# Reading K and V of two batches with the keys in another order: a source with 8 outer rows in place of 128

## The chip, the cores and the metric

The kernel runs on one core of a Trainium2 chip. The metric is the device time of one execution in microseconds; three runs of the kernel before have a median of 851.9 us. Lower is better. Times inside an execution are counted from the start of the profiled span.

## What is computed

Two attention blocks stand side by side, and their outputs are joined in the last dimension. Both have 16 batches of 32 query tokens, a model width of 1024, 32 query heads of width 128 and a cache of 1024 keys. Block A has 4 key/value heads, each shared by 8 query heads; block B has a key/value head for every query head. All inputs are bf16.

```python
q = (x @ wq).reshape(B, Sq, H, Dh).transpose(0, 2, 1, 3)
k, v = repeat(k_cache, rep, axis=1), repeat(v_cache, rep, axis=1)   # rep 8 in A, 1 in B
p = softmax(einsum("bhqd,bhkd->bhqk", q, k) * Dh ** -0.5)
o = einsum("bhqk,bhkd->bhqd", p, v)
out = o.transpose(0, 2, 1, 3).reshape(B, Sq, H * Dh) @ wo           # A and B, then concatenate
```

Softmax and the sum over keys don't depend on the order of the keys, as long as K and V have the same one.

## The kernel before

The program is written as a list of operations (matrix groups on TensorE, evictions from PSUM on VectorE or ScalarE, transfers issued by SyncE), each with the buffers that it reads and writes. A planner, `list_schedule`, gives every engine a fixed order, from a duration for each operation; a transfer's duration comes from its size (`dur`, in bytes) and its packets' length. Semaphores are put where an operation depends on one of another engine. SP carries all loads in one order, and waits before a load until the buffer that it overwrites is free.

The work of A runs in four blocks of heads, and in each block over the 16 batches in order: a batch brings one K tile and one V tile of A (1024 keys by 128, 256 KB), and its two halves (`q.half`) use them for 4 query heads each. So there are 64 K tiles and 64 V tiles of A in the run. Two buffers each hold them, by `q.b % 2` (`KA_sb`, `VA_sb`). Each is `[128 partitions, 8 chunks, 128]`, and partition p holds the keys 8p to 8p+7, 2 KB that lie together in DRAM:

- `st_dmaKA` (L885) and `st_dmaVA` (L892) issue the loads on SP.
- `st_ktrA` transposes the 8 chunks of K on TensorE (L963); the result is evicted to `KTA_sb`.
- `st_scoresA` multiplies by the queries (L989), `st_max` (L1029, VectorE) and `st_exp` (L1042, ScalarE) do the softmax's parts, `st_ptr` (L1054) transposes the probabilities, and `st_pvA` (L1074) multiplies them by V, chunk by chunk.

Chunk c of the transposed K therefore holds key 8p + c in column p, and chunk c of V has the same key on partition p.

Block B streams larger tiles: 512 KB for two heads, loaded at L904 (K) and L949 (V), in 4 KB rows. K of B is transposed on VectorE in place (L970), its scores are L1018 and its product with V is L1108. The weights of the queries (`wq`, L708) and of the outputs (`wo`, L789 and L799) are loaded between them. In the last steps some tiles of B are put into the buffers of `wq`, `xT` and `QT`, which are free by then.

Of the kernel before, what the change touches and what calls it, by code (L numbers as in the profile page):

```python
# [16 lines left out]
NVB_SLOTS = 6  # L17
XT_FREE = 54
LATE = 51
NQT = 5  # L20
NKB_SLOTS = 8
LAZY_PER_STEP = 100
# [524 lines left out]
def build(nc, pa, pb, out):  # L547
# [9 lines left out]
    NCH = Sk // P  # L557
# [22 lines left out]
    pr = Prog()  # L580
    stack = contextlib.ExitStack()
    with stack:
        def sb(name, shape, dt):
            return stack.enter_context(nc.sbuf_tensor(name, shape, dt))
# [9 lines left out]
        QT_sb = sb("QT_sb", [P, 2, Bn, HS, Sq], BF)  # L594
        Qtok = sb("Qtok", [P, NQT, CW], BF)
        QBt = sb("QBt", [P, CW], BF)
# [8 lines left out]
        KA_sb = sb("KA_sb", [P, 2, NCH, Dh], BF)  # L605
        VA_sb = sb("VA_sb", [P, 2, NCH, Dh], BF)
# [11 lines left out]
        def bank(v):  # L618
            return psum[:, v.idx, :]
# [17 lines left out]
        def evac(dst_ap, src_ap, reads, writes, name, eng=None, wtag=None, rtag=None, mul=None):  # L637
            def emit(e):
                dst = dst_ap() if callable(dst_ap) else dst_ap
                src = src_ap() if callable(src_ap) else src_ap  # L640
                if mul is not None:
                    if hasattr(e, "activation"):
                        return e.activation(dst, src, ACTF.Copy, scale=mul)
                    return e.tensor_scalar(dst, src, mul, None, ALU.mult)
                return e.copy(dst, src) if hasattr(e, "activation") else e.tensor_copy(dst, src)  # L645
            eng = eng or "any"
            pr.add(eng, emit, reads=reads, writes=writes, name=name if eng == "any" else name + "@" + eng, wtag=wtag, rtag=rtag)
# [66 lines left out]
        def wq_reads(pi, c, j0, j1):  # L714
            return [r_ for k_ in sorted(set(j * WQP // DJ for j in range(j0, j1))) for r_ in wq_res(pi, c, k_)]
# [22 lines left out]
        def qprojB(m_, G):  # L738
# [5 lines left out]
            for j0 in range(0, DJ, JS):  # L744
                def e_qp(e, j0=j0):
                    last = None
                    for j in range(j0, j0 + JS):
                        last = e.matmul(bank(v)[:, 0:CW], xT_sb[:, 1, j, G * P:(G + 1) * P], wq_sb[:, j, mh * CW:(mh + 1) * CW], start=(j == 0), stop=(j == DJ - 1))  # L748
                    return last
                ws = wq_reads(1, c2, j0, j0 + JS)  # L750
                pr.add("pe", e_qp, reads=ws + [("xT", 1, G)] + ([("xV", 0), ("xV", 1)] if m_ == NMSB - 1 else []), writes=[v], claims=[("Qtok", (m_ * NG + G) % NQT)], name="qprojB", dur=0.225 * JS,
                       rtag=dict((r_, ("wq", 1, c2)) for r_ in ws))
            qs = (m_ * NG + G) % NQT
            evac(Qtok[:, qs, :], lambda: bank(v)[:, 0:CW], reads=[], writes=[v, ("Qtok", qs)], name="qB_ev",
                 wtag={("Qtok", qs): (m_, G)}, mul=scale)

        def qprepB_tr(m_, G):
            qs = (m_ * NG + G) % NQT
            pr.add("dve", lambda e: e.transpose(QBt[:, :].bitcast(F32), Qtok[:, qs, :].bitcast(F32)),
                   reads=[("Qtok", qs)], writes=["QBt"], name="QBt_tr", rtag={("Qtok", qs): (m_, G)}, wtag={"QBt": (m_, G)})  # L760
# [103 lines left out]
        def mk_quadB(t):  # L864
# [13 lines left out]
            q.kid = ("B", t)  # L878
            return q

        def st_dmaKA(q):
            if not q.kv_new:
                return
            sl = q.kvslot
            pr.add("sp", lambda e: e.dma_start(KA_sb[:, sl, :, :], pa["k"][q.b, q.s].rearrange("(p c) d -> p c d", c=NCH)),  # L885
                   writes=[("KA", sl)], dma_key=f"ka{sl}", name="ka_dma", dur=Sk * Dh * 2, wtag={("KA", sl): q.kid})

        def st_dmaVA(q):
            if not q.kv_new:
                return  # L890
            sl = q.kvslot
            pr.add("sp", lambda e: e.dma_start(VA_sb[:, sl, :, :], pa["v"][q.b, q.s].rearrange("(p c) d -> p c d", c=NCH)),  # L892
                   writes=[("VA", sl)], dma_key=f"va{sl}", name="va_dma", dur=Sk * Dh * 2, wtag={("VA", sl): q.kid})

        def tile_src(key, x):
# [4 lines left out]
        def st_dmaKB(x):  # L900
            if x < 2 * NIT:
                kind, sl = home_k(x)
                pr.step, was = 2 * ((x - NKB) // 4) if x >= NKB else pr.step, pr.step
                pr.add("sp", lambda e: e.dma_start(tile_k(x), tile_src("k", x)), writes=[(kind, sl)], dma_key=f"{kind.lower()}{sl}", name="kb_dma",  # L904
                       dur=2 * Sk * Dh * 2, wtag={(kind, sl): x})
                pr.step = was

        V_LAST = 2 * NIT - 4

        XK = 4 * LATE + 4 + NKB  # L910
        XV = 4 * LATE + 4 + 2

# [33 lines left out]
        def st_dmaVB(x):  # L946
            kind, sl = home_v(x)
            pr.step, was = 2 * ((x - NVB) // 4) if x >= NVB else pr.step, pr.step
            pr.add("sp", lambda e: e.dma_start(tile_v(x), tile_src("v", x)), writes=[(kind, sl)],  # L949
                   dma_key=f"{kind.lower()}{sl}", name="vb_dma", dur=2 * Sk * Dh * 2, wtag={(kind, sl): ("V", x)})  # L950
            pr.step = was
# [48 lines left out]
        def st_scoresB(qs):  # L1000
            n = qs[0].pn
            vP, vPT = (("xT", 0, 0), ("xT", 0, 1)) if n >= XT_FREE and n % 2 else (Virt("P2"), Virt("PT2"))
            for q in qs:
                score_buf(q)
                q.vP, q.vPT, q.vO = vP, vPT, Virt("O2")
            q0 = qs[0]
            gp = (q0.m * NG + q0.G) % 2

            def e_s(e, fp):
                last = None  # L1010
                o0 = (fp // 2) * 64 + fp % 2
                for x in range(4):
                    for q in qs:
                        for g2 in range(2):
                            r0 = 32 * (2 * q.e + g2)
                            lhsT = QR[r0:r0 + 32, gp, 2 * q.bp + x // 2, x % 2, o0:o0 + 63:2]
                            rhs = tile_k(4 * q.pn + x)[r0:r0 + 32, :].rearrange("p (s x) -> p s x", s=16)[:, :, o0:o0 + 63:2]
                            last = e.matmul(bank(q.vS[g2])[32 * x:32 * x + 32, :].rearrange("p (s j) -> p s j", s=16), lhsT, rhs,  # L1018
                                            start=(fp == 0), stop=(fp == 3), tile_position=(r0, 32 * x))
                return last  # L1020
            qr = [("QR", gp, 2 * q0.bp + t_) for t_ in range(2)]
            kt = [(home_k(4 * q0.pn + x), ("T", 4 * q0.pn + x)) for x in range(4)]
            for fp_ in range(4):
                pr.add("pe", lambda e, fp_=fp_: e_s(e, fp_), reads=qr + [r_ for r_, _ in kt], writes=[r_ for q in qs for r_ in q.vS],
                       name="scoresB", tag="B%d" % q0.t, rtag=dict([(r_, (q0.m, q0.G)) for r_ in qr] + kt))
# [67 lines left out]
        def st_pvB(qs):  # L1093
            q0 = qs[0]
            vPT = q0.vPT
            gp = (q0.m * NG + q0.G) % 2
            vt = [home_v(4 * q0.pn + x) for x in range(4)]

            def e_pv(e, c0):
                last = None  # L1100
                pt = pt2_of(vPT).rearrange("p (m r two) -> p m r two", m=8, two=2)
                for c in range(c0, c0 + 4):
                    for t_ in range(2):
                        assert vt[2 * t_ + 1] == (vt[2 * t_][0], vt[2 * t_][1] + 1)
                        v2 = tiles_v(4 * q0.pn + 2 * t_, 2).rearrange("p i (s d) -> p i s d", s=16)
                        for q in qs:
                            e0, n0 = 64 * q.e, 64 * t_
                            last = e.matmul(bank(q.vbo)[n0:n0 + 64, 0:2 * Dh].rearrange("p (i d) -> p i d", i=2), pt[e0:e0 + 64, c // 2, n0:n0 + 64, c % 2],  # L1108
                                            v2[e0:e0 + 64, :, c, :], start=(c == 0), stop=(c == 15), tile_position=(e0, n0))
                return last  # L1110
            for c0 in range(0, 16, 4):
                pr.add("pe", lambda e, c0=c0: e_pv(e, c0), reads=[vPT] + vt, writes=[q.vbo for q in qs], claims=[("OT", 1, gp, h_) for h_ in range(MS)],
                       name="PVB", tag="B%d" % q0.t, rtag=dict((r_, ("V", 4 * q0.pn + x)) for x, r_ in enumerate(vt)))
# [88 lines left out]
        def pairB(n):  # L1202
# [6 lines left out]
            st_scoresB(qs)  # L1209
            while k_next[0] < min(2 * NIT, 4 * n + 4 + NKB + (4 if n >= LATE else 0)):  # L1210
                st_dmaKB(k_next[0])
# [11 lines left out]
            st_pvB(qs)  # L1223
            while v_next[0] < min(V_LAST, 4 * n + 4 + NVB + (4 if n >= LATE else 0)):
                st_dmaVB(v_next[0])
# [35 lines left out]
        for x in range(4):  # L1261
            st_dmaKB(x)
        st_dmaKA(quadsA[newA[0]])
        st_dmaVA(quadsA[newA[0]])
        for x in range(4):
            st_dmaVB(x)
# [86 lines left out]
        if SCHED:  # L1353
            pr = pr.list_schedule()
# [41 lines left out]
```

## Time and profile before

| | |
|---|---|
| three runs | 851.47, 851.9, 852.7 us |
| the profiled execution | 851.77 us |
| its span, first to last instruction | 850.0 us |
| granted TensorE clock in it | 0.998 |
| read from HBM | 337.6 MB |
| DMA packets | 112,208; 341.68 MB |
| loads of K and V of A | 64 and 64, 256 KB each, 8.4 and 8.7 us from issue to landing |
| loads of K and V of B | 256 and 256, 512 KB each |

The profile's page gives busy times of the engines, the span in 40 slices, the DMA queues, and the chain of work that ended last, followed back from the last instruction. In its groups a line reads: line, engine, operation, output <- inputs, count. Waits are given as who waited <- for whom: us in total, how often, the longest. The queue q1 carries the loads and stores that SP issues, q8 and q14 the instructions of the engines themselves, in blocks, and q0 the stores issued by GpSimd. The trace also holds every DMA packet with its start, length, size and queue, but not the number of its DMA engine, and the time of each semaphore increment: a transfer makes sixteen, and has landed with the last.

### The profile page before, as it was taken

Reading aid. Unit: us, or ns where it says so; the run is one execution under the profiler, and the core shown is the slowest. Engines: PE = TensorE matmul, PEld = TensorE weight load, DVE = VectorE, ACT = ScalarE, POOL = GpSimd, SP = SyncE. Lnnn points to the kernel's source line nnn. Section 1 sums busy time; section 2 is a strip of 40 time slices with the busy share of each in tenths; the row PEclk is TensorE's granted clock in tenths of the full one; section 3 lists DMA queues with packets and bytes.
Section 4 is the critical chain, followed back from the end, with each engine's and each line's share of the span. In section 5 each row is a group of like instructions: output and inputs, shape, how many; then the busy total and the mean of one; then the engine's idle time right before and its main releaser. Section 6 shows DMA issues by size and latency. Waiting matters only on the chain.

```text
span 850.0 us, 29762 instructions
## 1 busy us (share of the span) xinstructions
PE 781.1 (92%) x13056; PEld 519.9 (61%) x13056; DVE 734.1 (86%) x1025; ACT 622.9 (73%) x1356; POOL 6.1 (1%) x20
## 2 busy tenths in 40 slices
PE   6988989999899999999998998999999998989886
PEld 3456666666666566676565665566656666666654
DVE  1499898897898899998999789998899889998995
ACT  3378887876778767877777777686777758787864
POOL 1000000000000000000000000000000000000000
PEclk9999999999999999999999999999999999999999
DMA  9999999999999999999999999999999999999994
GB/s 331 415 404 411 412 411 416 415 400 354 409 414 411 415 412 411 415 397 413 408 416 414 413 406 403 415 403 414 413 404 411 410 411 407 416 415 414 416 417 187
DMA packets 112208, 341.68 MB, mean 402 GB/s; under 512 B 12048, under 2 KB 12304, under 8 KB 112080
## 3 DMA queue, kind: packets, MB, share of 16 engines
q1 hardware_dynamic: 111520, 337.95, 99.8%
q8 instruction: 103, 1.69, 0.7%
q0 software_dynamic: 560, 1.84, 0.5%
q14 instruction: 25, 0.20, 0.1%
HBM read 337.64 MB, written 2.10 MB: 400 GB/s over the span
## 4 chain that ended last, share of the span: by engine, by line
PE 53%; DVE 17%; DMA 15%; ACT 12%; issue 2%; SPq 1%; DVEq 0%; ACTq 0%
PE psum L1108 10%; PE psum L817 9%; DVE stat L1029 8%; ACT P_sb L1042 7%; DVE KB_sb L970 6%; DMA KB_sb<-in_B_k_cache_dram 6%; DMA VB_sb<-in_B_v_cache_dram 5%; PE psum L1018 5%; PE psum L1054 5%; PE psum L748 4%; PE psum L1088 4%; PE psum L989 4%; PE psum L729 4%; PE psum L1074 3%; PE psum L963 2%; DMA wq_sb<-in_B_k_cache_dram 2%
## 5 line engine op out<-in xcount | busy, mean ns | idle before, releaser
L1029 DVE TENSOR_REDUCE stat<-psum 128x1 f32<-128x1024 f32 x256 | 302.9, 1209 | 42.2 <-PE psum L989 25.3
L1042 ACT ACTIVATE P_sb<-psum,stat 128x1024 bf16<-128x1024 f32 x246 | 275.2, 1119 | 70.7 <-DVE stat L1029 67.8
L970 DVE STREAM_TRANSPOSE KB_sb<-KB_sb 128x1024 f32<-128x1024 f32 x240 | 289.7, 1226 | 17.3 <-DMA KB_sb<-in_B_k_cache_dram 16.8
L645 ACT COPY PT_sb<-psum 128x512 f32<-128x512 f32 x223 | 129.5, 598 | 39.7 <-PE psum L1088 22.2
L1108 PE MATMUL psum<-VB_sb,PT_sb 64*64 64x256 bf16 x3584 | 116.9, 271 | 11.9 <-ACT P_sb L1042 6.9
L1108 PEld LDWEIGHTS psum<-VB_sb,PT_sb 64*64 64x64 bf16 x3584 | 96.6, 107 | 33.0 <-issue 29.5
L1167 ACT ACTIVATE O_sb<-psum,stat 128x128 bf16<-128x128 f32 (+1 forms) x203 | 80.8, 418 | 35.4 <-PE psum L1074 16.1
L1054 PE MATMUL psum<-id,P_sb 128*128 128x128 f32 x512 | 88.5, 296 | 4.3 <-ACT P_sb L1042 3.0
L989 PE MATMUL psum<-KTA_sb,QT_sb 128*128 128x512 bf16 x256 | 82.0, 383 | 5.8 <-ACT P_sb L1042 2.6
L1054 PEld LDWEIGHTS psum<-id,P_sb 128*128 128x128 f32 x512 | 73.7, 208 | 19.5 <-ACT P_sb L1042 7.9
L1074 PE MATMUL psum<-VA_sb,PT_sb 128*128 128x128 bf16 x1024 | 77.8, 219 | 4.6 <-ACT P_sb L1042 1.9
L1088 PE MATMUL psum<-id,P_sb 128*128 128x128 f32 x472 | 78.1, 288 | 4.1 <-ACT P_sb L1042 1.1
L1074 PEld LDWEIGHTS psum<-VA_sb,PT_sb 128*128 128x128 bf16 x1024 | 62.5, 98 | 28.3 <-issue 12.3
L1018 PE MATMUL psum<-KB_sb,QR 32*32 32x512 bf16 x3840 | 72.7, 395 | 6.2 <-ACT P_sb L1042 5.4
L1088 PEld LDWEIGHTS psum<-id,P_sb 128*128 128x128 f32 x472 | 64.8, 193 | 20.1 <-ACT PT_sb L645 4.5
L748 PE MATMUL psum<-wq_sb,xT_sb 128*128 128x512 bf16 x256 | 73.0, 392 | 3.3 <-DMA wq_sb<-in_B_wq_dram 2.8
L817 PE MATMUL psum<-woB_sb,OTB_sb 128*128 128x512 bf16 x256 | 66.3, 380 | 3.6 <-ACT P_sb L1042 1.6
L817 PE MATMUL psum<-woA_sb,OTA_sb 128*128 128x512 bf16 x256 | 62.8, 380 | 2.2 <-ACT P_sb L1042 1.9
L1018 PEld LDWEIGHTS psum<-KB_sb,QR 32*32 32x32 bf16 x3840 | 43.6, 89 | 32.5 <-ACT P_sb L1042 9.8
L729 PE MATMUL psum<-xT_sb,wq_sb 128*128 128x512 bf16 x192 | 53.3, 379 | 0.5 <-ACT P_sb L1042 0.3
L1042 ACT ACTIVATION_READ_ACCUMULATOR P_sb<-psum,stat 128x1 f32 x246 | 49.6, 202 | 0.0
L829 DVE TENSOR_TENSOR acc<-acc,psum 128x512 f32<-128x512 f32 x64 | 41.2, 674 | 4.2 <-PE psum L817 4.2
(74 smaller groups left out, 718.3 us busy)
## 6 DMA issues: line engine op xcount, KB each, us to landing
KB_sb<-in_B_k_cache_dram SPq DMA_DIRECT2D x240, 512.0 KB, 9.6
VB_sb<-in_B_v_cache_dram SPq DMA_DIRECT2D x234, 512.0 KB, 9.2
KA_sb<-in_A_k_cache_dram SPq DMA_DIRECT2D x64, 256.0 KB, 8.4
VA_sb<-in_A_v_cache_dram SPq DMA_DIRECT2D x64, 256.0 KB, 8.7
wq_sb<-in_B_wq_dram SPq DMA_DIRECT2D x16, 512.0 KB, 8.1
woB_sb<-in_B_wo_dram SPq DMA_DIRECT2D x32, 256.0 KB, 9.8
woA_sb<-in_A_wo_dram SPq DMA_DIRECT2D x32, 256.0 KB, 10.0
wq_sb<-in_B_k_cache_dram SPq DMA_DIRECT2D x16, 512.0 KB, 11.4
```

The lines of the kernel that those rows point to most:

```text
L645: return e.copy(dst, src) if hasattr(e, "activation") else e.tensor_copy(dst, src)
L748: last = e.matmul(bank(v)[:, 0:CW], xT_sb[:, 1, j, G * P:(G + 1) * P], wq_sb[:, j, mh * CW:(mh + 1) * CW], start=(j == 0), stop=(j == DJ - 1))
L817: last = e.matmul(bank(v)[:, 0:OUTW], OT[:, gp, hh, :], wo_[:, hh, oh * OUTW:(oh + 1) * OUTW], start=(hh == 0), stop=(hh == nh - 1))
L970: pr.add("dve", lambda e: e.transpose(tile_k(x).bitcast(F32), tile_k(x).bitcast(F32)), writes=[home_k(x)], name="KBt_tr", rtag={home_k(x): ...
L989: pr.add("pe", lambda e, u=u: e.matmul(bank(vS[u]), qt[:, q.b, q.hh0:q.hh0 + 4, :].rearrange("p a q -> p (a q)"), KTA_sb[:, sl, u * 512:(u ...
L1018: last = e.matmul(bank(q.vS[g2])[32 * x:32 * x + 32, :].rearrange("p (s j) -> p s j", s=16), lhsT, rhs, start=(fp == 0), stop=(fp == 3), t ...
L1029: pr.add("dve", lambda e: e.tensor_reduce(stat[:, vst.idx, 0:1], both(vS), AXIS.XY, ALU.max, negate=True), writes=vS + [vst], name="max")
L1042: return e.activation(dst, src, ACTF.Exp, bias=stat[:, vst.idx, 0:1], scale=1.0, accum_out=stat[:, vst.idx, 1:2])
L1054: last = e.transpose(bank(vb)[:, m * P:(m + 1) * P], p32[:, m:Sk // 2:NPK], id32[:])
L1074: last = e.matmul(bank(vb)[:, 0:Dh], ptc_of(vPT, c, 0, P), VA_sb[:, kvs, c, :], start=(c == 0), stop=(c == NCH - 1))
L1088: last = e.transpose(bank(vb)[:, m * P:(m + 1) * P], p32[:, 4 * h + m:Sk:8], id32[:])
L1108: last = e.matmul(bank(q.vbo)[n0:n0 + 64, 0:2 * Dh].rearrange("p (i d) -> p i d", i=2), pt[e0:e0 + 64, c // 2, n0:n0 + 64, c % 2], v2[e0:e ...
```

## The change

For the batches b with b % 8 == 3 (3 and 11), the K and V tiles of A are read with the keys in another order. With x from 0 to 7 and v from 0 to 15, partition 16x + v gets the keys 64v + 8x to 64v + 8x + 7. The source is then an array with 8 outer rows (a step of 2 KB), 16 inner ones (a step of 16 KB) and 2 KB that lie together. K and V have the same order, so the result stays. The destination is written as 128 partitions of 1024 numbers for all batches. Nothing else is changed; sizes, buffers, waits and names are as before.

```diff
+EIGHT = (3,)
...
+        def a_src(key, q):
+            src = pa[key][q.b, q.s]
+            if q.b % 8 in EIGHT:
+                return src.rearrange("(v x c) d -> x v (c d)", x=8, c=NCH)
+            return src.rearrange("(p c) d -> p (c d)", c=NCH)
+
         def st_dmaKA(q):
...
-            pr.add("sp", lambda e: e.dma_start(KA_sb[:, sl, :, :], pa["k"][q.b, q.s].rearrange("(p c) d -> p c d", c=NCH)),
+            pr.add("sp", lambda e: e.dma_start(KA_sb[:, sl, :, :].rearrange("p c d -> p (c d)"), a_src("k", q)),
                    writes=[("KA", sl)], dma_key=f"ka{sl}", name="ka_dma", dur=Sk * Dh * 2, wtag={("KA", sl): q.kid})
 
         def st_dmaVA(q):
...
-            pr.add("sp", lambda e: e.dma_start(VA_sb[:, sl, :, :], pa["v"][q.b, q.s].rearrange("(p c) d -> p c d", c=NCH)),
+            pr.add("sp", lambda e: e.dma_start(VA_sb[:, sl, :, :].rearrange("p c d -> p (c d)"), a_src("v", q)),
                    writes=[("VA", sl)], dma_key=f"va{sl}", name="va_dma", dur=Sk * Dh * 2, wtag={("VA", sl): q.kid})
```

## The prediction

> **What bounds the kernel now.** I read the page first: engines, DMA rows, chain.
>
> ```profile
> PE 781.1 (92%) x13056; PEld 519.9 (61%) x13056; DVE 734.1 (86%) x1025; ACT 622.9 (73%) x1356; POOL 6.1 (1%) x20
> DMA  9999999999999999999999999999999999999994
> q1 hardware_dynamic: 111520, 337.95, 99.8%
> q8 instruction: 103, 1.69, 0.7%
> PE 53%; DVE 17%; DMA 15%; ACT 12%; issue 2%; SPq 1%; DVEq 0%; ACTq 0%
> KA_sb<-in_A_k_cache_dram SPq DMA_DIRECT2D x64, 256.0 KB, 8.4
> VA_sb<-in_A_v_cache_dram SPq DMA_DIRECT2D x64, 256.0 KB, 8.7
> ```
>
> TensorE is 92% busy and the DMA engines are busy from end to end: two limits of nearly one height. The waits and the chain say which of them counts where. Waits for a landing, from 60 to 570 us and then from 570 us to the end (us in total, times, longest):
>
> ```profile
> DVE KB_sb L970 <- DMA KB_sb<-in_B_k_cache_dram: 11.8, 16, 2.0
> PE psum L1108 <- DMA VB_sb<-in_B_v_cache_dram: 2.6, 5, 0.7
> PE psum L817 <- DMA woB_sb<-in_B_wo_dram: 0.4, 1, 0.4
> ```
>
> So 14.8 us of waiting, in pieces of about 0.7 us, and almost all before 570 us. The chain (start, us, what) still passes through a transfer every 16 to 140 us, and the last one is what the end hangs on:
>
> ```profile
> 102.47 7.99 DMA VB_sb<-in_B_v_cache_dram
> 140.08 9.15 DMA VB_sb<-in_B_v_cache_dram
> 167.01 12.71 DMA KB_sb<-in_B_k_cache_dram
> ...
> 553.90 6.19 DMA KB_sb<-in_B_k_cache_dram
> 686.25 9.94 DMA woB_sb<-in_B_wo_dram
> 812.16 14.65 DMA wq_sb<-in_B_k_cache_dram
> 826.84 1.25 DVE wq_sb L970
> ```
>
> The last K tile lands at 826.81 us, DVE takes it at once, and 23 us of work follow to 850.0.
>
> **What a landing waits for.** A transfer has landed when its sixteen semaphore increments are in. For that last K tile they come at 821.89 us plus 0, 0.02, 0.15, 0.51, 0.78, 0.96, 1.02, 1.20, and then 2.92, 2.93, 3.42, 3.57, 3.74, 3.92, 4.27, 4.92 us: eight DMA engines are through early, eight run behind, and the last sets the landing. The median spread over all transfers is 3.3 us. The packet records say why. Packets of one engine follow each other at a fixed pitch (2 KB every 80 ns, 4 KB every 155 ns), so each can be tied to the one that starts where it ended. Besides the data there are the 103 instruction blocks of 16 KB (q8 above, 0.935 us each); their lengths repeat with a period of eight, so they go round eight engines, and the two that I could measure alone threw their engine back by 1.41 and 1.40 us. Over the run that is 103 / 8 x 1.41 = 18.1 us on each of eight engines and none on the other eight.
>
> **The change, part by part.** Dependences, sizes and the planner's durations (`dur=Sk*Dh*2`) stay, so all five instruction orders stay. No instruction is added on PE, DVE or ACT: the keys' order inside a tile differs, but K and V share it.
>
> *The transfers.* Batches 3 and 11 are read once in each of four blocks: 8 K and 8 V transfers, 16 in all. Every transfer of before uses 16 engines (11,936 closing packets for 746 transfers), 8 packets of 2 KB each here, 0.646 us. One with an outermost 8 is not in the trace. Two ends: it is dealt over 16 as before and nothing changes, or its eight groups go to eight engines, 16 packets each. I take eight, since the dealing goes by rows now and there are eight outer ones. An engine then needs 1.29 us: the row for it is the weight load of wq, 16 packets of 2 KB per engine, which land 1.29 us apart, and which also step through DRAM with gaps (2 KB of every 8 KB), as the new source does (2 KB of every 16 KB). So each transfer puts 0.646 us more on eight engines and takes 0.646 us from the others: 16 x 0.646 = 10.3 us each way.
>
> [...]
>
> *Which eight.* In the first transfer eight increments come within 0.08 us, the other eight 0.47 to 0.66 us later: engines are served in two halves. Three of the later half then idle for 2 us and stay 1.7 us behind the rest; the first instruction block (23.4 us) falls on one of these three. The second and third fall on engines that a stall at 54 us puts into the same later half: there eight engines stop after 4 or 5 of a transfer's 8 packets, the other eight after 3 or not at all. So the blocks ride on the half that is served second. A transfer that needs only eight is nearest to the row in which the first half is served first; I take that half, the free one.
>
> *The sum.* Loaded engines: 18.1 - 10.3 = 7.8 us behind an ideal one; free engines: 0 + 10.3. The larger falls from 18.1 to 10.3: 7.8 us less, the most that can come of it. The least is nothing: where queues run dry (185 to 210 us, and about 54, 370, 550, 625 and 700 us) compute sets the pace and the lag is reset. For what counts I take the stretches separately. After the dry point at 700 us the chain's end is a landing: one K and one V transfer of batch 11 (issued at 730 and 755 us) lie in it, 2 x 0.646 = 1.3 us off the last engine, whole on the path. Before that, 6.5 us of relief remain, and 14.8 us of waits in short pieces, about eleven of them on the chain (11 x 0.67 = 7.4 us); behind each of them PE's own order is late next. I take 0.3 of the 6.5, 2.0 us, because PE is 92% busy. Together 3.3 us: the profiled execution took 851.77 us (span 850.0), 0.1 below the median of 851.9, so 848.6.
>
> *Costed at nothing.* The changed transfers themselves land up to 0.65 us later on the free engines. Between landing and first use (L963 for K, L1074 for V) the 64 K tiles have a median of 15 us and the 64 V tiles 9.3; of the sixteen the tightest is a V at 477.8 us, used 1.35 us later. If the slack were gone it would cost 0.65 us each. SP's issues (0.33 to 0.45 us) may grow for a three-level source; SP spends some 430 us waiting for PE to free buffers, so 16 x 0.2 us hide there, and what queues behind is the next load with 8 to 10 us to its landing.
>
> **Rivals.**
>
> *The eight are the loaded ones (slower).* Then 18.1 + 10.3 = 28.4 us on the worst half. For it: no view names an engine, and my tying rests on three blocks. Against: three out of three. It decides from the first pair on (40 us), since that half is already the last. At the same share of what reaches the path (3.3 of 7.8) 10.3 us give 4.4: 856.2. Chance 0.15.
>
> *The eight get in others' way (slower).* Each of eight engines writes a run of 16 partitions, where now each writes eight. If packets slow as far as the slowest in the trace, the instruction blocks (16 KB in 0.935 us against 0.62 for four of 4 KB, a factor 1.5), a transfer takes 1.93 us: the free half gets 16 x 1.29 = 20.6 us, over the 18.1 of now, and the others' gain goes in the collisions. It decides from a factor of 1.38 (16 x 0.646 x (2 x 1.38 - 1) = 18.1). 2.5 us, in jumps of 2.6 us per pair, which I count in full: 854.3. Against: strided 2 KB packets in wq keep 80 ns. Chance 0.14.
>
> [...]
>
> *Hidden anyway (no change).* Compute sets the time everywhere but in the tail, and there the V tiles, landing at 839.87 us and used at 840.49, keep the end. 851.5. For: no wait of note after 570 us. Against: the chain's last link but DVE's is a landing. Chance 0.10.
>
> *It doesn't do what it says.* All 16 engines are used still: 851.9. Chance 0.02.
>
> **Numbers.** The forecast has 0.59. A measurement of this kernel tells about 0.2%, 1.7 us, from no change. Faster by more: 0.59; within: 0.10 + 0.02 = 0.12; slower: 0.15 + 0.14 = 0.29. The likeliest case's own range is 844.1 (all 7.8 us) to 850.6 (the tail alone). The range cuts little off below, 845.0, and reaches the loaded-half case, 856.2, above.
>
> **What would show it.** Right: the packet count stays 112,208 but the sixteen transfers' engines close with 16 data packets; the two groups of eight increments close up, with a spread at the last K landing under 3.5 us instead of 4.9; that landing comes before 825.5 us; the waits of L970 for KB fall under 9 us. Wrong in its half: the spread grows to 6 us or more. Wrong in its pace: increments of KA and VA of these batches, or those behind them, more than 1.4 us apart from their neighbours on one engine. Wrong in the share: the landings move forward, but PE's waits take the time back.

## The result: 29 us slower

The changed kernel takes 880.81 us (four runs, 879.68 to 882.32), the one before 851.69 in the same set of runs. The ratio is 1.0341, 95% interval 1.0321 to 1.036: slower by 3.4%. The profiled execution took 880.12 us, 878.3 of it in the span. Here and below a difference in microseconds is the ratio less one, times the median of before in the same set; here 0.0341 x 851.69 = 29.0.

Engines, DMA rows and chain of the profile after:

```profile
PE 787.8 (90%) x13056; PEld 523.1 (60%) x13056; DVE 736.8 (84%) x1025; ACT 623.1 (71%) x1356; POOL 6.1 (1%) x20
DMA  9999999999999999999999999999999999999994
DMA packets 112080, 341.68 MB, mean 389 GB/s; under 512 B 11920, under 2 KB 12176, under 8 KB 111952
q1 hardware_dynamic: 111392, 337.95, 99.5%
q8 instruction: 103, 1.69, 0.7%
PE 46%; DMA 25%; DVE 14%; ACT 10%; SPq 2%; issue 2%; DVEq 0%; ACTq 0%
KA_sb<-in_A_k_cache_dram SPq DMA_DIRECT2D x64, 256.0 KB, 9.2
VA_sb<-in_A_v_cache_dram SPq DMA_DIRECT2D x64, 256.0 KB, 9.4
```

The packets before:

```profile
DMA packets 112208, 341.68 MB, mean 402 GB/s; under 512 B 12048, under 2 KB 12304, under 8 KB 112080
```

Same bytes, and the DMA engines as busy as before, for 28 us longer: they move less in their busy time (389 GB/s, 402 before). 128 packets are missing, 16 x 8: each changed transfer closes on eight engines in place of sixteen. Nearly every kind of load takes longer to land (the 240 K tiles of B 10.4 us, 9.6 before), and the chain passes through transfers for 25% of the span, before 15%.

The longest waits for a landing from 60 to 570 us (us in total, times, longest; the lines of the loads and behind them have moved by 7, L817 by 1), and below from 570 us to the end:

```profile
DVE KB_sb L977 <- DMA KB_sb<-in_B_k_cache_dram: 27.1, 27, 3.0
PE psum L1115 <- DMA VB_sb<-in_B_v_cache_dram: 4.3, 3, 2.8
PE psum L818 <- DMA woB_sb<-in_B_wo_dram: 2.9, 2, 2.2
```

```profile
DVE KB_sb L977 <- DMA KB_sb<-in_B_k_cache_dram: 7.0, 12, 1.2
PE psum L1115 <- DMA VB_sb<-in_B_v_cache_dram: 3.2, 2, 2.8
```

34.3 us in the first stretch where 14.4 had been, and 10.2 in the second, which had 0.4. Transfers of B, which the change doesn't touch, are nearly all of the late ones: for tiles of A, TensorE waits 1.7 us in both stretches together, before not at all. From the chain (start, us, what):

```profile
427.23 10.27 DMA VB_sb<-in_B_v_cache_dram
458.29 9.28 DMA KB_sb<-in_B_k_cache_dram
482.86 13.58 DMA VA_sb<-in_A_v_cache_dram
...
820.42 14.74 DMA KB_sb<-in_B_k_cache_dram
835.18 1.25 DVE KB_sb L977
```

The link at 482.86 us is a changed transfer, the one at 458.29 was issued 0.7 us behind a changed one (K, 457.61 us). That one by stretches (stretch, its length, busy us of each engine, granted clock, DMA share, GB/s):

```profile
455.00:460.00 5.00, 4.76 (x113) 3.54 (x111) 5.00 (x8) 4.73 (x11) 0.00 (x0) 1.00 1.01 413
460.00:463.00 3.00, 2.12 (x28) 1.48 (x31) 3.00 (x4) 2.81 (x7) 0.00 (x0) 1.00 0.98 298
463.00:464.00 1.00, 1.00 (x44) 1.00 (x42) 1.00 (x3) 1.00 (x3) 0.00 (x0) 1.00 1.01 401
464.00:466.00 2.00, 2.00 (x40) 1.39 (x29) 1.51 (x5) 2.00 (x6) 0.00 (x0) 1.00 1.08 336
466.00:471.00 5.00, 3.25 (x26) 1.90 (x24) 3.54 (x6) 2.21 (x5) 0.00 (x0) 1.00 1.02 407
```

Twice the rate falls, to 298 and to 336 GB/s, with the DMA engines busy all the time. The trace's semaphore increments tell why twice. The transfer ahead, the changed one and the one behind (us):

```
ahead    459.98 460.04 460.10 460.19 460.30 460.32 460.36 460.42 460.55 460.72 461.46 461.61 462.30 462.41 464.01 464.69
changed  462.14 462.27 462.42 462.44 462.62 462.77                                                         465.84 466.61
behind   462.99 463.04 463.09 463.17 463.44 463.48 463.51 463.67 463.68 463.69 463.70 463.72 463.94 464.03 466.99 467.57
```

Six of the eight engines do their part between 460 and 462.8 us; the other two are the two that were last already, and do it from 464 us on. And in both stretches the 4 KB packets are long, also those of engines that have no part in the changed transfer: their median is 159 ns from 456 to 460 us, 211 in the microsecond from 461, 159 again at 462 and 463, 213 and 208 from 464 and 465, and 159 from 466 on; a few last over 1 us. All 67 that start from 464.75 to 465.75 us last 194 ns or more. So there are two things to explain: packets that lengthen on every engine, and the last engine's double work. Summed over all engines from 20 us on, what data packets last beyond 159 ns (4 KB) and 84 ns (2 KB) is 176 engine-us in the profile before and 582 after. The rise is bunched at the sixteen changed transfers: 342 of the 582 lie in the 110 us in which these are carried out (each from 2.4 us before its first engine's increment to 0.2 us behind the last), and the other 750 us have 240. Divided by sixteen engines the rise is 406 / 16 = 25.4 us. Below this rise, so divided, is called the lengthening of a run.

TensorE's granted clock fell too: 0.986 to 0.990 in the four runs, 0.998 in the profile before. In the profile after it stands at a half four times, for 17.0 us in all (from 76.2, 287.8, 472.1 and 694.0 us), and in the four microseconds ahead of each TensorE had been idle for 2.0 to 2.8 us; before, it stands at a half once within the work, for 3.4 us. TensorE's busy time grew by 6.7 us (781.1 to 787.8), half of the 13.6 us more. Ahead of 472.1 us the chain leads from the late K tile above (landed at 467.57 us) over DVE and ACT to TensorE, idle from 469.2 to 471.2 us. So up to some 6.7 of the 29 us may be a slower TensorE behind longer waits; no run here tells this part from the rest.

### The profile page after: what moved, and what is told of

Same layout as the page of the kernel before. It is cut to its first block, busy times and chain, and to the rows that moved or that the text cites. A ratio compares the mean times of both kernels' runs of the same rounds, so it can differ in the third digit from the quotient of the medians.

```text
span 878.3 us, 29762 instructions
## 1 busy us (share of the span) xinstructions
PE 787.8 (90%) x13056; PEld 523.1 (60%) x13056; DVE 736.8 (84%) x1025; ACT 623.1 (71%) x1356; POOL 6.1 (1%) x20
## 4 chain that ended last, share of the span: by engine, by line
PE 46%; DMA 25%; DVE 14%; ACT 10%; SPq 2%; issue 2%; DVEq 0%; ACTq 0%
DMA KB_sb<-in_B_k_cache_dram 16%; PE psum L818 8%; PE psum L1115 8%; ACT P_sb L1049 6%; DVE stat L1036 6%; DVE KB_sb L977 5%; DMA VB_sb<-in_B_v_cache_dram 5%; PE psum L1025 5%; PE psum L1061 4%; PE psum L730 4%; PE psum L1095 4%; PE psum L749 3%; PE psum L996 3%; PE psum L1081 3%; PE psum L970 2%
## 5 line engine op out<-in xcount | busy, mean ns | idle before, releaser
L977 DVE STREAM_TRANSPOSE KB_sb<-KB_sb 128x1024 f32<-128x1024 f32 x240 | 291.3, 1230 | 38.8 <-DMA KB_sb<-in_B_k_cache_dram 38.3
L1115 PE MATMUL psum<-VB_sb,PT_sb 64*64 64x256 bf16 x3584 | 120.1, 276 | 18.5 <-ACT P_sb L1049 7.5
L1115 PEld LDWEIGHTS psum<-VB_sb,PT_sb 64*64 64x64 bf16 x3584 | 99.2, 109 | 39.8 <-issue 36.3
## 6 DMA issues: line engine op xcount, KB each, us to landing
KB_sb<-in_B_k_cache_dram SPq DMA_DIRECT2D x240, 512.0 KB, 10.4
```

The costliest lines, as they stand in the source:

```text
L977: pr.add("dve", lambda e: e.transpose(tile_k(x).bitcast(F32), tile_k(x).bitcast(F32)), writes=[home_k(x)], name="KBt_tr", rtag={home_k(x): ...
```

## Experiments

Three theories of the lengthening and the lateness: *writes* (a source with few outer rows gives each engine a run of neighbouring partitions, which takes it to where other engines write), *reads* (2 KB of every 16 KB, read side by side), *load* (eight engines simply have double work). In all runs the orders of PE, DVE, ACT and POOL are those of before.

**Other reading, same outer 8.**

```diff
-                return src.rearrange("(v x c) d -> x v (c d)", x=8, c=NCH)
+                rows = pa[key].rearrange("b s (g c) d -> (b s g) (c d)", c=NCH)[128 * (4 * q.b + q.s):]
+                return rows[:136].rearrange("(x v) e -> x v e", x=8)[:, :16]
```

> The sixteen transfers keep an outermost source dimension of 8, but each engine now reads sixteen adjacent 2 KB pieces, and the next engine starts 34 KB further on (17 pieces, so that the two source dimensions can't be merged; up to 7 of the 128 pieces of these two batches come from the tile behind, and the keys of these batches are other ones). Writes theory (what slows all engines is that each of eight writes a run of 16 partitions, out of its usual place): unchanged, 881. Reads theory (it is the reading of 2 KB every 16 KB by engines that walk side by side): the lengthened packets go, and the time is between my forecast and before, 848.6 to 852. Load theory (eight engines simply have double the work, and they are the wrong eight): 881 as well, with the spread of the increments as in the changed kernel.

880.03 us, ratio 1.0335 (1.0311 to 1.0358); lengthening 23.8 us. Each engine reads 32 KB that lie together, and nothing is gained. The reads theory falls; the other two had both forecast this.

**Strided reading, outer 128.**

```diff
-                return src.rearrange("(v x c) d -> x v (c d)", x=8, c=NCH)
+                n = 4 * q.b + q.s
+                return pa[key].rearrange("b s (g c) d -> (b s g) (c d)", c=NCH).rearrange("(r p j) e -> r j p e", p=128, j=8)[n // 8, n % 8]
```

> The sixteen transfers keep an outermost dimension of 128 and so sixteen engines in their usual dealing; only the source steps by 16 KB per partition (one piece of 2 KB out of each 16 KB, over eight tiles; the keys of these two batches are other ones). Reads theory: as slow as the changed kernel or slower, 875 to 885, since all sixteen engines read with the step. Writes theory and load theory: 852, as before.

851.68 us, ratio 1.0015 (0.9998 to 1.0033); lengthening 0.1 us. The step of 16 KB costs nothing that shows.

**The old order in two halves.**

```diff
+            return [e.dma_start(dst[h:h + 64], src[h:h + 64]) for h in (0, 64)] if cut else e.dma_start(dst, src)
```

> The sixteen transfers in their old key order, each as two transfers of 64 partitions (0 to 63, then 64 to 127) on one semaphore: sixteen engines, four packets each per half, nothing strided. If every engine takes four neighbouring partitions of a half, engines no longer stand in their usual places. Writes theory: two engines meet at one place, each transfer takes its 0.646 us twice, 16 x 0.646 = 10.3 us, 862. Reads and load theory: 852, but for 16 more issues on SP at 0.35 us, which lie in SP's waiting. [...]

872.35 us, ratio 1.0239 (1.0213 to 1.0264): 20.3 us, with a lengthening of 20.5. No step in the source, the old key order, and still two thirds of the whole loss, where the load theory had forecast 852: it can't be all of it. The writes theory had the sign right and forecast half of the size.

**Outer 16.**

```diff
-                return src.rearrange("(v x c) d -> x v (c d)", x=8, c=NCH)
+                return src.rearrange("(v x c) d -> x v (c d)", x=16, c=NCH)
```

> As the change, with an outermost dimension of 16 in place of 8: sixteen engines, eight packets each, a run of eight neighbouring partitions per engine, the source stepping by 32 KB inside an engine and by 2 KB between engines. Load theory: 852, since all sixteen have the same work again. Writes theory: two engines meet at one place, 16 x 0.646 = 10.3 us, 862. Reads theory: sixteen engines side by side with a step, at least as slow as the changed kernel, 881 or more.

869.02 us, ratio 1.0207 (1.019 to 1.0224): 17.6 us, lengthening 16.5. I took sixteen outer rows to give all sixteen engines equal work (no view names an engine). So 17.6 of the 29.0 us are there where load had forecast nothing and writes 10.3. What remains for the eight is 11.4.

**Eight engines on partitions 0 to 63, and on 64 to 127.** Each run loads only half of these tiles. The two differ only in the numbers 0, 32 and 64, 96:

```diff
+            return [e.dma_start(dst[h:h + 32], src[h:h + 32].rearrange("(v x) e -> x v e", x=8)) for h in (0, 32)] if cut else e.dma_start(dst, src)
```

> Each of the sixteen transfers loads only partitions 0 to 63, in two transfers of 32 partitions with an outermost 8 (key order (v x), v=4, x=8 inside each quarter); partitions 64 to 127 of these tiles are left out and keep older keys. Eight engines then have 2 x 4 = 8 packets, the work that they have today, and eight have none. Writes theory: each of the eight stays at its usual place, no packet is lengthened, and the time is between 846 (the loaded half is the one relieved, 10.3 us of 18.1) and 852 (it is not). Load theory: the same range. [...]

> As the run with partitions 0 to 63 alone, but with partitions 64 to 127 loaded and 0 to 63 left out: the same number of engines, transfers, packets and bytes, the same key order inside a quarter; only the partitions that the eight engines write are other ones. Load theory: the same time as that run, within 1 us. Writes theory: now each of the eight writes where one of the other eight writes too; by the measured 20.5 engine-us per transfer cut into two halves of 64 partitions, one such half costs some 10, so 16 x 10 / 16 = 10 us more than that run, 856 to 862.

Partitions 0 to 63: 850.42 us, ratio 0.9996 (0.9976 to 1.0017), lengthening 1.8 us. Partitions 64 to 127: 865.14 us, ratio 1.0174 (1.0121 to 1.0227), 14.8 us (10.3 to 19.3), above the 856 to 862 that writes had forecast; lengthening 13.9. Number of engines, packets, bytes and order of reading are equal; the place that is written makes some 15 us. (The half of the tile that is read is another one too, but neither run on reading found a price for it.) The wait of L970 over the whole run before, and of L977 first for partitions 0 to 63, then for 64 to 127:

```profile
DVE KB_sb L970 <- DMA KB_sb<-in_B_k_cache_dram: 16.8, 19, 3.3
```

```profile
DVE KB_sb L977 <- DMA KB_sb<-in_B_k_cache_dram: 12.1, 15, 3.7
```

```profile
DVE KB_sb L977 <- DMA KB_sb<-in_B_k_cache_dram: 21.8, 26, 3.7
```

Only the writes theory had set these two runs apart: the place that is written counts. (That both runs use the same eight engines is taken from their equal shapes; no view names an engine. That the other eight are the ones that write partitions 64 to 127 in a transfer of 128 was my assumption and was not shown.)

The first of the two shows something else. Eight engines were relieved of 10.3 us each, and the time stayed. That has two readings: the engines relieved were not the ones that set the landings, or the landings came earlier and the compute engines took the time back. The wait of L977 fell (16.8 to 12.1 us), and so did the transfers' share of the chain, from 15% to 6%:

```profile
PE 57%; DVE 19%; ACT 15%; DMA 6%; issue 3%; SPq 1%; DVEq 0%; ACTq 0%
```

So some landings did come earlier, and this run alone doesn't decide; the runs under "Who is last" do.

**The load shift without the meetings.** As the runs above, with two more part-transfers into rows of the output:

```diff
+            return [e.dma_start(d_, src[h:h + 32].rearrange("(v x) e -> x v e", x=8)) for d_, h in ((dst[:32], 0), (dst[32:64], 32), (out_flat[384:416, D:2 * D], 64), (out_flat[416:448, D:2 * D], 96))] if cut else e.dma_start(dst, src)
```

> The load shift of the change without its meeting writes: each of the sixteen transfers goes as four of 32 rows with an outermost 8, so eight engines get 4 x 4 = 16 packets and eight get none. Two of the four write partitions 0 to 63 of the tile; the other two write their 128 KB into rows of the output in DRAM that are written properly at the end (so partitions 64 to 127 of these tiles keep older keys). Writes theory: no lengthened packets in SBUF, and the time of my forecast's own sum, 848.6 if the eight are the free half, 856 if they are the loaded one. Load theory: as slow as the changed kernel, 875 to 881. If writes to DRAM slow the others, that shows as lengthened packets.

861.88 us, ratio 1.0114 (1.0079 to 1.015): 9.7 us (6.7 to 12.8), with a lengthening of 3.8. Neither of the two numbers of writes, and not the load theory's. Within that interval eight engines with sixteen packets cost what the shift puts on them, 16 x 0.646 = 10.3, in full; a part may be the lengthening.

**All of the work, in quarters.**

```diff
+            return [e.dma_start(dst[h:h + 32], src[h:h + 32].rearrange("(v x) e -> x v e", x=8)) for h in (0, 32, 64, 96)] if cut else e.dma_start(dst, src)
```

> The whole change's work in an order in which the eight engines stand on eight different groups of four partitions at any time: four transfers of 32 partitions with an outermost 8 each, key order (v x), v=4, x=8 inside a quarter, 16 packets per engine. [...] Writes theory: only the last two quarters cost, some 10 engine-us per transfer, 16 x 10 / 16 = 10 us: 859 to 862. Load theory: as the changed kernel, 881, since the eight have the same sixteen packets. Three more issues per transfer cost SP 16 x 3 x 0.4 = 19 us, inside its 430 us of waiting.

874.39 us, ratio 1.026 (1.0223 to 1.0297): 22.1 us (19.0 to 25.3). I had some 10 and had left the load out; its lengthening of 13.0 us and the 10.3 us of load make 23.3.

**Who is last.** The trace names no DMA engine, but in the run on partitions 0 to 63 the eight can be found by matching times. Each part-transfer needs 0.33 us, so their sixteen increments must be eight of the preceding transfer's sixteen, plus 0.33 and plus 0.66 us; in every one of the sixteen places a choice fits with 0.13 to 0.48 us of misfit over all sixteen values (choices that differ in one early engine often fit nearly as well). In the ten places from 340 us on, the last engine of the core is one of them eight times; in the six before 270 us it never is, which fits the shorter waits of that run. At the V transfer of 662.7 us, for one, the eight stand 0, 0.13, 0.17, 0.28, 0.51, 0.52, 2.35 and 2.93 us behind the first. (In the kernel after, in all ten changed transfers from 350 us on, two of the eight land 2.1 us or more behind the sixth, as in the table above.) An instruction block shows as one engine that falls back by 1.41 us, so it can be seen too whether a block hits one of the eight. Numbered from 0 and taken modulo eight, blocks 6 and 7 hit one of the eight in seven cases of seven, blocks 1, 3 and 4 one of the others in six of six, block 2 one of the others in three of four (0 and 5 had no case near enough). By these few cases two of the engines that carry blocks belong to the eight that a transfer with eight outer rows uses, and most of the others do not. The two runs that follow test this without any reading of increments:

```diff
+            return [e.dma_start(dst, src), e.dma_start(out_flat[384:448, D:2 * D], src[:64].rearrange("(v x) e -> x v e", x=8))] if cut else e.dma_start(dst, src)
```

and the same with `384:416`, `src[:32]` and `x=4`.

> The kernel of before, its sixteen transfers as they were, and beside each a second one on the same semaphore: 64 pieces of 2 KB with an outermost 8 from the same tile into rows of the output in DRAM, which are written properly at the end. So eight engines get 8 packets more per transfer, 16 x 0.646 = 10.3 us in all, and nothing meets in SBUF. New theory (two of the eight engines that any such transfer uses are among those that carry the instruction blocks, and the last engine sets every landing): 10.3 us more, 860 to 863, like the run with the shifted load. My forecast's theory (the eight are all free): 852, since 10.3 us stay under the 18.1 us by which the others are behind. A theory of bytes alone: 2 MB more over sixteen engines, 5.2 us, 856.

> As the run with the extra transfers of 8, but the extra transfer has an outermost 4 and 32 pieces: four engines get the same 8 packets more per transfer, 10.3 us in all on each of these. New theory: 851 to 853 if neither block-carrying engine of the eight is among these four, 860 to 863 if one is. Forecast's theory: 852. Bytes alone: 1 MB, 2.6 us, 854.5. [...]

Outer 8: 858.88 us, ratio 1.0121 (1.0088 to 1.0153), 10.3 us (7.5 to 13.0; the medians alone differ by 8.3), no lengthening. Outer 4: 851.64 us, ratio 1.0016 (1.0005 to 1.0027), 1.4 us (0.4 to 2.3). Both lie outside what bytes alone would give (5.2 and 2.6 us). Eight packets more, sixteen times, 10.3 us for each engine, are paid in full within the interval when eight engines get them and nearly free when four do. (That four outer rows go to four engines was taken from the kernel after, where eight close on eight.) Had the eight been free by 18.1 us, the first would have cost nothing. So engines that set the end are among the eight and, by the second run, not among those four. The transfers' shares of the chain point the same way (15% before), first of the run with 8, then of that with 4:

```profile
PE 48%; DVE 18%; DMA 17%; ACT 12%; issue 3%; SPq 2%; DVEq 0%; ACTq 0%
```

```profile
PE 49%; DVE 20%; DMA 13%; ACT 13%; issue 3%; SPq 1%; DVEq 0%; ACTq 0%
```

## Why the prediction was wrong, step by step

*Eight engines, sixteen packets, 0.646 us each way.* Right: nine increments in place of sixteen per transfer (eight engines and one at once), and 16 x 0.646 = 10.3 us lies in the middle of what the run with extra transfers of 8 measured (7.5 to 13.0).

*Which eight.* This step failed first. Three blocks out of three lay on the later half, and I took all 103 to do so, and the eight to be the free ones. Three observations of a pattern with period eight left five places unseen, and two of those lie on two of the eight. A landing waits for the last engine: to relieve the other eight of 10.3 us brings nothing (the run on partitions 0 to 63: 850.4), and 10.3 us more on the eight cost about as much, because of the loaded ones among them. The gain of 3.3 us became a loss of some 10.

*The share of the path.* I took 0.3 of a relief before 700 us, and 3.3 of 7.8 us, also for a loss. A loss on the last engines is paid whole or nearly: 7.5 to 13.0 us for 10.3. A relief was not paid at all where waits did get shorter (L977 16.8 to 12.1 us on partitions 0 to 63). The first alone put the rival of the loaded eight at 856.2 where the run with the extra transfers has 860.9 (850.6 x 1.0121; its median is 858.9).

*"The eight get in others' way".* This is the larger miss: the forecast's own sum had nothing for it, and the rival had 2.5 us at a chance of 0.14. The rival was right that the written place counts (850.4 us on partitions 0 to 63, 865.1 on 64 to 127), and its term was mis-sized, 2.5 us for 17.6 (outer 16, where load had forecast nothing). I let only the sixteen transfers' own packets lengthen, by 1.5, a transfer taking 1.93 us, and that part held: in the table above the two last engines need 1.83 and 1.92 us. But the packets of the other transfers lengthen with them: 4 KB packets by 208 / 159 = 1.3 to 213 / 159 = 1.34 in the places above, twice per transfer there, since two of the eight come late. Per transfer that is 25.4 engine-us, against 0.646 x 16 = 10.3 for all its data.

*"Strided 2 KB packets in wq keep 80 ns".* True, and the run with outer 128 bears it out (85.8 ns mean, 85.5 before), but it speaks of reads only. The wq loads write 128 partitions in the outermost place, as the loads of K and V before do, so no row of the profile before could speak for or against the meetings; the argument should have left the factor open to above.

*Costed at nothing.* Right in the main. SP's issues rose to 0.63 to 0.76 us (one to 1.07), and the two runs with one more issue per transfer and no other price pay nothing for it that shows (850.4 and 851.6). The slack of the tiles of A was a small part of the price: from 60 us on, TensorE's waits for them grew from 0 to 1.7 us, where the waits for B shown above grew by 29.7.

*What would show it.* The packet count does not stay: I forgot that eight engines close with eight packets fewer. The spread at the last K landing went from 4.92 to 5.93 us, just under the 6 that I gave for the wrong half; that landing moved from 826.81 to 855.16 us, and L977 waits 38.3 us for KB where under 9 was forecast (16.8 over the whole run before).

*The sum.* Outer 16 and the load shift, each from its own run: 17.6 + 10.3 = 27.9 (the second is good to some 3 us), measured 29.0. Both may hold some of the slower TensorE behind longer waits. By lengthening: 25.4 + 10.3 = 35.7, too much, so part of the lengthening must fall on engines that have slack. Which part was not measured, and why packets of engines with no part in the changed transfers lengthen too stays open; that halves of 64 partitions cost twice what the writes theory had for them (20.3 for 10.3) belongs to the same question. No run was faster than before: relieving the eight that such a transfer doesn't use leaves the last two, and none of these layouts relieves those.

## What to carry to other kernels

Beside a stream that keeps all DMA engines busy, keep 128 outermost on both sides of a transfer: here sixteen transfers of 746 with 16 outer rows cost 17.6 us and with 8 cost 29.0, and the price fell on the transfers around, not on the changed one alone (4 KB packets of 159 ns lasted 208 to 213). Before work is moved between DMA engines, find the last engine and prove which set it is in: here 10.3 us less on each of eight engines left the time at 850.4 us (850.5 before), and 10.3 us more on each of eight cost 7.5 to 13.0. A pattern with period eight is not read from three cases.

## What the runs showed of the hardware

- Sixteen loads of 256 KB with eight or sixteen outer rows, or in halves of 64 partitions, cost the whole stream 16.5 to 25.4 engine-us of longer packets each; with eight outer rows every 4 KB packet that started in the microsecond from 464.75 us lasted 194 ns or more (the median is 159 at 463 us and from 466 us on). 128 KB loaded in two transfers with eight outer rows cost 1.8 engine-us into partitions 0 to 63 and 13.9 into 64 to 127.
- With eight outer rows a transfer's issue takes SP 0.63 to 0.76 us in fifteen cases of sixteen (0.33 to 0.43 before, one 0.53).
- The lengths of the 103 instruction blocks (0.935 us in the mean before) repeat with a period of eight. Two of the eight DMA engines that would carry them seem to be among the eight on which a transfer with eight outer rows closes, by times that were matched. Sixteen extra transfers of 64 pieces of 2 KB with eight outer rows cost 10.3 us (7.5 to 13.0), of 32 pieces with four outer rows 1.4 (0.4 to 2.3).
- TensorE's granted clock stood at a half for 3.4 us or 6.8 us at a time, four times, behind idle times of 2.0 to 2.8 us.
